# Second product of a fused Mamba-2 and feed-forward kernel: operands exchanged, so that its outputs come by tokens

## Chip, core and metric

The kernel runs on one core of one Trainium2 chip. The metric is device microseconds of one execution, the median of repeated runs: 374.59 us before the change (three runs, 374.59 to 374.6). Engines are named TensorE (PE in the profile, with PEld for its weight loads), VectorE (DVE), ScalarE (ACT), GpSimd (POOL) and SyncE (SP). A trailing q (SPq, ACTq) is an engine's own instruction queue.

## What is computed

```python
# block 1: mamba2_ssd on x (4, 8, 768, 32), a (4, 8, 768), B and C (4, 8, 768, 16)
#   per chunk:  y = (C B^T * L) x  +  (C state) * decay ;  state = decay * state + sum(B x decay)
x = attn_out.transpose(0, 2, 1, 3).reshape(3072, 256)      # 3072 tokens, d_model 256
# block 2: feed-forward, w_in (256, 2048), w_out (2048, 256), float64 in memory
h = x @ w_in
g = h * (1.0 / (1.0 + np.exp(-1.702 * h)))
out = (g @ w_out).astype(np.float32)
```

The kernel works in fp32. It computes g as Silu(1.702 h), which is 1.702 times too large, and puts the factor 1/1.702 (`1.0 / GELU_SCALE`) into the end of the second product.

## The kernel before

**Groups.** The 3072 tokens are taken in six groups of 512 (NG = 6, numbered 0 to 5 in the code; the change concerns 1 to 5). For each group the Mamba block gives `yT` (features on partitions, tokens along the free dimension), the first product gives `gT[g, j]` for eight blocks j of 256 hidden units, and the second product, `product(g, j)`, accumulates the outputs over the eight blocks. Group 0 uses plain products (`hidden`, `half`, `project_all`), the first product of group 1 is plain too.

**Seven products for eight.** The second product of groups 1 to 5, and the first product of groups 2 to 5, use the Strassen-Winograd scheme: a 2x2 block product made with seven block products. The sums of the operands are made by VectorE: `mix_w` for the weights (kept), `mix_y` for the first product, and `mix_g(g, j)` (lines 699 to 703) for the block `gT[g, j]`, four sums of 128x256 in three instructions. `product` (line 809) then issues seven matmuls per block, numbered by `ORDER`. The weights are the stationary operand (128x128), gT or its sums the moving one, 256 tokens wide. Each accumulator is therefore 128 output features by 256 tokens. The seven lie in one four-bank PSUM area, `area(f"acc{g}")`, of a pool with one buffer. The same buffer is used by `score(p)` (line 538), the matmuls of the Mamba block's scores, whose result VectorE multiplies into the decays with `weigh(p)` (L557).

**Combining.** When a group's products are done, `combine(g)` (line 849) makes the four output blocks: `copies` (one ScalarE instruction, L840, takes two accumulators to SBUF), then five VectorE additions through `plus` (line 846; all additions are told as L847 in the profile, also those of the first product's chains). The result `c` has features on partitions.

**Transposing.** `give(g)` (line 867) turns that result by eight TensorE transposes of 128x128 (`turn_out`, L864) into two PSUM banks of the general pool, lets ScalarE copy them to `ob` with the factor 1/1.702 (L872), and stores 2 x 256 KB through SyncE's queue (L761).

**Order.** Every engine executes its instructions in the order in which the code emits them. The order around the change is written out by hand in strings that `run` (line 1076) executes: "2.1" is step 1 of the first product's chain for block 2 (`first`, L733 and L743; the letters D, T and S are its VectorE and ScalarE steps), "P" is the next single product of the list given, s1 and s2 are scores, w1 and w2 their weighings, y1 and y2 the `finish` of a Mamba pair, M0 to M2 are mixings. In line 1121 the last products of the group before are interleaved with the first chains of the next group, and `C` is `combine(g - 1)`. In lines 1136 and 1137 the scores s1 follow; `give` stands after w1. In group 5, which has no more Mamba work, `give(4)` stands at line 1155, after the run.

**Closing stretch.** `end(5, 5)` (line 876) does the last three blocks of group 5, ordered by accumulator, so that the combining runs beside the products; the last accumulator's products are split into two halves of 128 tokens, to let the last additions begin. Then three sets of transposes, three scalings (L912, L915 on ScalarE, L918 on VectorE) and three stores (L761, and L883 on two queues).

Of the kernel before, what the change touches and what calls it, by code (L numbers as in the profile page):

```python
# [8 lines left out]
FP32 = mybir.dt.float32  # L9
# [7 lines left out]
P = 128  # L17
# [18 lines left out]
def kernel(  # L36
# [450 lines left out]
    def bank(name):  # L487
        return ps.tile([P, 4 * P], FP32, tag="ff", name=name)
# [49 lines left out]
    def score(p, to=None):  # L538

        s = st[p]  # L540
        BT, CT = s.pop("BT"), s.pop("CT")
        cb = (area(f"cb{p}") if to is None else to).rearrange("p r (k e) -> p r k e", k=2)
        for k, r in [(k, r) for r in range(R) for k in range(2)] if to is not None else [
                (k, r) for k in range(2) for r in range(R)]:
            rows = slice(32 * r, 32 * r + 32)
            nc.tensor.matmul(out=cb[:, r, k], lhsT=BT[rows, k],  # L546
                             rhs=CT[rows, k].rearrange("p q i -> p (q i)"),
                             start=True, stop=True, tile_position=(32 * r, 0),
                             skip_group_check=True)
        s["cb"] = cb  # L550
# [207 lines left out]

    def store(g, half, ob):
        r0 = g * TG + half * HT  # L760
        nc.sync.dma_start(out=out[r0:r0 + HT, :].rearrange("(k p) d -> p k d", p=P), in_=ob)  # L761

    def out_tile(g, half):
        return ffn.tile([P, 2, DM], FP32, tag="ob", name=f"ob{g}_{half}", bufs=2)
# [17 lines left out]

    mixed_w, mixed_g, acc, done = {}, {}, {}, {}

    def mix_w(n):

# [17 lines left out]

    ORDER = (0, 1, 5, 4, 2, 3, 6)

    def product(g, j, only=ORDER, cols=slice(0, HT)):
        if j == 0 and g not in acc:  # L810
            if g < NG - 1:
                a = area(f"acc{g}").rearrange("p r (t e) -> p (r t) e", t=2)
                acc[g] = [a[:, i] for i in range(7)], a
            else:

                areas.close()
                last = ctx.enter_context(
                    tc.tile_pool(name="last", bufs=1, space=bass.MemoryType.PSUM))
                tiles = [last.tile([P, 2, HT], FP32, name=f"acc{g}_{i}") for i in range(4)]
                acc[g] = [tiles[i // 2][:, i % 2] for i in range(7)], tiles  # L820
        B = gT[g, j].rearrange("p i (t e) -> p i t e", t=2)
        T = mixed_g[g, j]
        A, S = w_out[:, 2 * j:2 * j + 2], mixed_w[j]

        terms = ((A[:, 0, :P], B[:, 0, 0]), (A[:, 1, :P], B[:, 1, 0]), (S[:, 1], T[:, 2]),
                 (S[:, 0], T[:, 0]), (S[:, 2], T[:, 1]), (S[:, 3], B[:, 1, 1]),
                 (A[:, 1, P:], T[:, 3]))
        for i in only:
            lhsT, rhs = terms[i]
            nc.tensor.matmul(out=acc[g][0][i][:, cols], lhsT=lhsT, rhs=rhs[:, cols],  # L830
                             start=(j == 0 and i in (0, 2, 5, 6)), stop=(j == NF // 2 - 1),
                             skip_group_check=True)

    def copies(g):
        u = ffn.tile([P, 4, HT], FP32, tag="gT", name=f"u{g}", bufs=6)
        c = ffn.tile([P, 2, 2, HT], FP32, tag="gT", name=f"c{g}", bufs=6)
        done[g] = u, c

        if g < NG - 1:
            nc.scalar.activation(u[:, 0:4:3], acc[g][1][:, 0:4:3], AF.Copy)  # L840
        else:
            nc.scalar.activation(u[:, 0], acc[g][0][0], AF.Copy)
            nc.scalar.activation(u[:, 3], acc[g][0][3], AF.Copy)
        return u, c

    def plus(o, v, w):
        nc.vector.tensor_tensor(out=o, in0=v, in1=w, op=ALU.add)  # L847

    def combine(g):


        u, c = copies(g)
        a = acc[g][1]
        plus(u[:, 2], a[:, 2], u[:, 0])
        plus(u[:, 1:3], a[:, 3:5], u[:, 2:3].to_broadcast([P, 2, HT]))
        plus(c[:, 1, 1], u[:, 2], u[:, 3])
        plus(c[:, 0], a[:, 1:6:4], u[:, 0:2])
        plus(c[:, 1, 0], a[:, 6], u[:, 2])

    def turn_out(g, t, blocks, o, ks=range(2)):  # L860

        for i in blocks:
            for k in ks:
                nc.tensor.transpose(out=o[:, k, i * P:(i + 1) * P],  # L864
                                    in_=done[g][1][:, i, t, k * P:(k + 1) * P], identity=ident)

    def give(g):
        for t in range(2):
            o = bank(f"oT{g}_{t}").rearrange("p (k e) -> p k e", k=2)
            turn_out(g, t, range(2), o)  # L870
            ob = out_tile(g, t)
            nc.scalar.activation(ob, o, AF.Copy, scale=1.0 / GELU_SCALE)  # L872
            store(g, t, ob)
        done.pop(g)

    def end(g, j0):

        def products(i, cols=slice(0, HT)):
            for j in range(j0, NF // 2):
                product(g, j, (i,), cols)  # L880

        def put(k0, k1, i, ob, queue):
            queue.dma_start(  # L883
                out=out[g * TG + HT + k0 * P:g * TG + HT + k1 * P, i * P:(i + 1) * P].rearrange(
                    "(k p) d -> p k d", p=P), in_=ob[:, k0:k1])

        _, p2, p6, p5, p7, p3, p4 = acc[g][0][:7]
        products(0)
        products(3)
        u, c = copies(g)  # L890
        u2, u4, u3 = u[:, 2], u[:, 1], c[:, 1, 0]
        products(4)
        products(2)
        plus(u2, p6, u[:, 0])
        plus(u4, p5, u2)
        products(6)
        plus(u3, p7, u2)
        plus(c[:, 1, 1], u3, u[:, 3])
        products(1)
        plus(c[:, 0, 0], p2, u[:, 0])  # L900
        o = [bank(f"oT{g}_{i}").rearrange("p (k e) -> p k e", k=2) for i in range(3)]
        ob = [ffn.tile([P, 2, TG], FP32, tag="gT", name=f"ob{g}_1_{i}", bufs=6)[:, :, :P]
              for i in range(2)]
        halves = [slice(k * P, (k + 1) * P) for k in range(2)]
        products(5, halves[0])
        plus(c[:, 1, 0], p4, u3)
        plus(c[:, 0, 1, halves[0]], p3[:, halves[0]], u4[:, halves[0]])
        products(5, halves[1])
        plus(c[:, 0, 1, halves[1]], p3[:, halves[1]], u4[:, halves[1]])
        turn_out(g, 0, range(2), o[0])  # L910
        half_out = out_tile(g, 0)
        nc.scalar.activation(half_out, o[0], AF.Copy, scale=1.0 / GELU_SCALE)  # L912
        store(g, 0, half_out)
        turn_out(g, 1, (1,), o[2])
        nc.scalar.activation(ob[1], o[2][:, :, P:], AF.Copy, scale=1.0 / GELU_SCALE)  # L915
        put(0, 2, 1, ob[1], nc.scalar)
        turn_out(g, 1, (0,), o[1])
        nc.vector.tensor_single_scalar(out=ob[0], in_=o[1][:, :, :P], scalar=1.0 / GELU_SCALE,  # L918
                                       op=ALU.mult)
        put(0, 2, 0, ob[0], nc.sync)  # L920


    assert PG == 2
# [152 lines left out]
    def run(g, steps, products=(), **do):  # L1076


        products = iter(products)
        for step in steps.split():  # L1080
            if step == "P":
                product(*next(products))
            elif step in do:
                do[step]()
            else:
                j, i = step.split(".")
                first(g, int(j), i)
        assert next(products, None) is None

    def seven(g, j):  # L1090
        return [(g, j, (i,)) for i in ORDER]
# [17 lines left out]
    for g in range(2, NG):  # L1109
# [23 lines left out]

        if more:

            run(g, "2.1 1.S 1.4 1.3 2.6 2.5 2.2 2.7 1.T s1 2.D 2.S w1 give 2.4 3.1 2.3 3.5 2.T M0 3.6 "
                "s2 w2 y1 refill 3.7 3.2 3.D along 4.1 P P 3.4 P 3.S 4.6 P 3.3 4.5 3.T M1 P P y2 4.7 P 4.2 4.D M2",
                seven(g, 0), s1=lambda: score(n), w1=lambda: weigh(n), give=lambda: give(g - 1),
                s2=lambda: score(n + 1), w2=lambda: weigh(n + 1), y1=lambda: finish(n),
                refill=refill, along=along, y2=lambda: finish(n + 1), M0=lambda: mix_g(g, 0), M1=lambda: mix_g(g, 1),  # L1140
                M2=lambda: mix_g(g, 2))
            if most:
                decay(chunks[0])
        else:
            run(g, "2.1 1.S 1.4 1.3 2.6 2.5 2.2 2.7 1.T 2.D M0 3.1 3.5 2.S 2.4 3.6 2.3 3.2 3.7 2.T 3.D M1",
                M0=lambda: mix_g(g, 0), M1=lambda: mix_g(g, 1))
# [5 lines left out]
        k = NF // 2 - 1  # L1152
        run(g, f"P {k}.S P {k}.4 P P {k}.3 {k}.T P P P", seven(g, 4))
        if not more:
            give(g - 1)
            for j in range(k - 1, k + 1):
                mix_g(g, j)
            break
# [37 lines left out]
```

## Time and profile before

| | before |
|---|---|
| time, median of 3 | 374.59 us |
| span of the profiled execution | 373.0 us |
| transposes of outputs, L864 | 40, in five runs of eight, starting at 157.42, 214.46, 271.50, 357.13 and 367.77 us |
| passes of the second product, L830 | 566 (two per fp32 matmul) |
| additions with 128x512 at L847, gT<-Y,ac | 32, mean 691 ns |
| copies of transposed outputs, ScalarE L872 | eight in four pairs, a pair takes 1.08 us |
| stores of 256 KB, out_dram<-ob | 11, median 2.4 us from issue to landing |
| DMA, mean over the span | 79 GB/s |

How to read it: a matmul in fp32 appears as two weight loads and two MATMUL records. Matmuls are pipelined, so the duration of a record (its latency) is longer than the distance between two starts, and "busy" is no measure of how well the array is used. The times at the left of a timeline are microseconds from the start of the span; a group's first number is the start of its first instruction and the second the length from there to the end of the last. In brackets stands how long the engine sat idle, and who released it.

### The profile page before, as it was taken

The numbers are of one execution on the slowest core, as the hardware profiler recorded it, in microseconds if no ns is written. First come the engines' busy times: TensorE is split into PE (matmuls) and PEld (weight loads), VectorE is DVE, ScalarE is ACT, GpSimd is POOL, SyncE is SP. The second block draws the span as 40 slices with busy tenths as digits, with TensorE's granted clock in tenths as the row PEclk, the third lists the DMA queues.
The fourth block names the chain that finished last, engine by engine and source line by source line (L and its number), as shares of the span: only waits on it lengthen the run. The fifth ranks groups of instructions, "written<-read, shape, count | busy, mean of one in ns | idle before, by whom it ended". The sixth has DMA issues, their size and how long they took to land.

```text
span 373.0 us, 5764 instructions
## 1 busy us (share of the span) xinstructions
PE 364.5 (98%) x2278; PEld 285.1 (76%) x2278; DVE 267.6 (72%) x439; ACT 151.9 (41%) x337; POOL 10.9 (3%) x34
## 2 busy tenths in 40 slices
PE   8999999999999999999999999999999999999995
PEld 3674468885467588778888788888878888888884
DVE  4999999998879976587886475888484355464443
ACT  5678661402331123553433554433554331554320
POOL 4200000100000010000000000000000000000000
PEclk9999999999999999999999999999999999999999
DMA  9997799706856110086300073000010000000011
GB/s 151 240 335 128 241 215 140 239 18 106 191 143 112 58 42 0 2 155 128 113 2 1 0 128 100 0 2 0 0 58 2 0 3 1 0 2 0 0 58 56
DMA packets 85794, 29.56 MB, mean 79 GB/s; under 512 B 75720, under 2 KB 79240, under 8 KB 85768
## 3 DMA queue, kind: packets, MB, share of 16 engines
q1 hardware_dynamic: 83320, 28.81, 32.8%
q10 hardware_dynamic: 2448, 0.39, 0.6%
q8 instruction: 18, 0.29, 0.3%
q14 instruction: 8, 0.07, 0.1%
HBM read 25.95 MB, written 3.24 MB: 78 GB/s over the span
## 4 chain that ended last, share of the span: by engine, by line
PE 91%; DVE 5%; ACT 2%; DMA 1%; issue 1%; ACTq 0%; DVEq 0%
PE acc L830 33%; PE X L733 13%; PE h L661 13%; PE Y L743 10%; PE o L773 8%; PE cb L546 3%; PE y L619 3%; DVE c L847 2%; PE y L610 2%; PE h L675 1%; PE ab L462 1%; PE tp L498 1%; DVE u L847 1%; PE oT L864 1%; ACT L L481 1%; PE A L574 1%
## 5 line engine op out<-in xcount | busy, mean ns | idle before, releaser
L830 PE MATMUL acc<-mg,mw 128*128 128x256 f32 x240 | 66.0, 379 | 0.0
L847 DVE TENSOR_TENSOR gT<-Y,ac 128x512 f32<-128x512 f32 x32 | 22.1, 691 | 44.3 <-PE Y L743 42.4
L738 ACT ACTIVATE ac<-X 128x256 f32<-128x256 f32 x64 | 24.5, 383 | 66.5 <-PE X L733 66.5
L830 PEld LDWEIGHTS acc<-mg,mw 128*128 128x128 f32 x240 | 45.6, 190 | 6.2
L661 PE MATMUL h<-yT,w_in 128*128 128x512 f32 x112 | 49.9, 595 | 0.0
L710 ACT ACTIVATE gT<-gT 128x512 f32<-128x512 f32 x64 | 33.3, 520 | 28.2 <-DVE gT L847 27.8
L830 PE MATMUL acc<-gT,w_out 128*128 128x256 f32 x160 | 43.8, 380 | 0.0
L347 DVE TENSOR_TENSOR_SCAN L<-a,idents 128x1024 f32<-128x1024 f32 x18 | 41.1, 2283 | 0.0
L733 PE MATMUL X<-my,mi 128*128 128x256 f32 x128 | 38.7, 384 | 0.0
L661 PEld LDWEIGHTS h<-yT,w_in 128*128 128x128 f32 x112 | 20.8, 190 | 23.4 <-issue 21.4
L830 PEld LDWEIGHTS acc<-gT,w_out 128*128 128x128 f32 x160 | 30.2, 190 | 5.5 <-issue 1.4
L847 DVE TENSOR_TENSOR gT<-Y,b 128x256 f32<-128x256 f32 x32 | 13.5, 422 | 26.7 <-PE Y L743 26.4
L664 ACT ACTIVATE gT<-h 128x512 f32<-128x512 f32 x28 | 16.6, 596 | 39.4 <-PE h L661 39.3
L773 PE MATMUL o<-w_out,gT 128*128 128x256 f32 x128 | 29.0, 382 | 0.0
L701 DVE TENSOR_TENSOR mg<-gT 128x512 f32<-128x512 f32 x40 | 27.3, 682 | 0.0
L733 PEld LDWEIGHTS X<-my,mi 128*128 128x128 f32 x128 | 23.7, 190 | 4.3 <-issue 1.2
L773 PEld LDWEIGHTS o<-w_out,gT 128*128 128x128 f32 x128 | 23.8, 190 | 4.1 <-issue 1.1
L557 DVE TENSOR_TENSOR L<-L,cb 128x2048 f32<-128x2048 f32 (+1 forms) x12 | 25.3, 2107 | 1.7 <-PE cb L546 1.6
L830 PE MATMUL acc<-gT,mw 128*128 128x256 f32 (+1 forms) x86 | 24.1, 369 | 0.4 <-DVE c L847 0.4
L830 PE MATMUL acc<-mg,w_out 128*128 128x256 f32 x80 | 23.5, 379 | 0.0
L641 ACT ACTIVATE yT<-y 128x256 f32<-128x256 f32 x22 | 7.2, 381 | 35.6 <-PE y L619 35.3
L733 PE MATMUL X<-yT,w_in 128*128 128x256 f32 x64 | 19.3, 383 | 0.0
(144 smaller groups left out, 540.5 us busy)
## 6 DMA issues: line engine op xcount, KB each, us to landing
a<-scratch SPq DMA_DIRECT2D x18, 512.0 KB, 5.6
bits<-in_moe_w_out_dram SPq DMA_DIRECT2D x4, 1024.0 KB, 7.3
x<-in_x_dram SPq DMA_DIRECT2D x24, 128.0 KB, 3.5
out_dram<-ob SPq DMA_DIRECT2D x11, 256.0 KB, 2.4
bits<-in_moe_w_in_dram SPq DMA_DIRECT2D x4, 512.0 KB, 5.8
bits<-in_moe_w_in_dram SPq DMA_DIRECT2D x2, 1024.0 KB, 9.4
b<-in_B_dram SPq DMA_DIRECT2D x24, 64.0 KB, 3.5
c<-in_C_dram SPq DMA_DIRECT2D x22, 64.0 KB, 2.5
```

Source lines behind the costliest of these rows:

```text
L347: nc.vector.tensor_tensor_scan(out=Ls[p][:, k].rearrange("p r q i -> p (r q i)"), data0=ra[n], data1=idents.rearrange("p h i -> p (h i)"), ...
L557: nc.vector.tensor_tensor(out=Lv[:, k], in0=Lv[:, k], in1=cb.rearrange("p r k e -> p k r e")[:, k], op=ALU.mult)
L661: nc.tensor.matmul(out=h, lhsT=w_in[:, k, f * P:(f + 1) * P], rhs=yT[g][:, k], start=(k == 0), stop=(k == NK - 1))
L664: nc.scalar.activation(gT[g, j][:, i], h, AF.Silu, scale=GELU_SCALE)
L701: nc.vector.tensor_tensor(out=t[:, 0:2], in0=B[:, :, 1], in1=B[:, 0], op=ALU.subtract)
L710: nc.scalar.activation(o, i, AF.Silu, scale=GELU_SCALE)
L733: nc.tensor.matmul(out=s["X"], lhsT=lhsT, rhs=rhs, start=i == "1", stop=i == "4", skip_group_check=True)
L738: nc.scalar.activation(copy, s["X"], AF.Copy)
L743: nc.tensor.matmul(out=o, lhsT=lhsT, rhs=rhs, start=s.pop("new", False), stop=i != "5", skip_group_check=True)
L773: nc.tensor.matmul(out=o[k // 2][:, k % 2], lhsT=gT[g, f // 2][:, f % 2, k * P:(k + 1) * P], rhs=w_out[:, f], start=(f == 0 and k % 2 == 0 ...
L830: nc.tensor.matmul(out=acc[g][0][i][:, cols], lhsT=lhsT, rhs=rhs[:, cols], start=(j == 0 and i in (0, 2, 5, 6)), stop=(j == NF // 2 - 1), ...
L847: nc.vector.tensor_tensor(out=o, in0=v, in1=w, op=ALU.add)
```

## The change

In groups 1 to 5 the two operands of each second product change places: a block of 128 tokens of gT (or of its sums) becomes the stationary operand, and the 128 columns of w_out (or its sums) the moving one. Each product of 256 moving columns thus becomes two of 128. The accumulators, and so the combined outputs, have tokens on partitions, as the output in memory has. So the transposes, their copies and the tiles for them go away; the result of the combining is stored directly. The factor 1/1.702 goes into the copies of `copies` (as ScalarE's scale) and into the additions that read PSUM (`scaled`, a scalar_tensor_tensor in place of a tensor_tensor). The order of the additions in `combine` changes by one: the sum that reads no PSUM comes last. In `end` the split into halves goes, the block of the last accumulator that is ready first is stored earlier, and the first half of the group is stored ahead of the last products.

```diff
@@ -758,7 +758,9 @@
     def store(g, half, ob):
         r0 = g * TG + half * HT
-        nc.sync.dma_start(out=out[r0:r0 + HT, :].rearrange("(k p) d -> p k d", p=P), in_=ob)
+        o = out[r0:r0 + HT, :]
+        nc.sync.dma_start(out=o.rearrange("(k p) d -> p k d", p=P) if len(ob.shape) == 3 else
+                          o.rearrange("(k p) (c d) -> p k c d", p=P, c=2), in_=ob)
     def out_tile(g, half):
         return ffn.tile([P, 2, DM], FP32, tag="ob", name=f"ob{g}_{half}", bufs=2)
@@ -806,7 +808,7 @@
     ORDER = (0, 1, 5, 4, 2, 3, 6)
-    def product(g, j, only=ORDER, cols=slice(0, HT)):
+    def product(g, j, only=ORDER):
         if j == 0 and g not in acc:
             if g < NG - 1:
                 a = area(f"acc{g}").rearrange("p r (t e) -> p (r t) e", t=2)
@@ -826,98 +828,81 @@
                  (S[:, 0], T[:, 0]), (S[:, 2], T[:, 1]), (S[:, 3], B[:, 1, 1]),
                  (A[:, 1, P:], T[:, 3]))
         for i in only:
-            lhsT, rhs = terms[i]
-            nc.tensor.matmul(out=acc[g][0][i][:, cols], lhsT=lhsT, rhs=rhs[:, cols],
-                             start=(j == 0 and i in (0, 2, 5, 6)), stop=(j == NF // 2 - 1),
-                             skip_group_check=True)
+            w, h = terms[i]
+            for k in range(2):
+                cols = slice(k * P, (k + 1) * P)
+                nc.tensor.matmul(out=acc[g][0][i][:, cols], lhsT=h[:, cols], rhs=w,
+                                 start=(j == 0 and i in (0, 2, 5, 6) and k == 0),
+                                 stop=(j == NF // 2 - 1), skip_group_check=True)
     def copies(g):
         u = ffn.tile([P, 4, HT], FP32, tag="gT", name=f"u{g}", bufs=6)
-        c = ffn.tile([P, 2, 2, HT], FP32, tag="gT", name=f"c{g}", bufs=6)
-        done[g] = u, c
+
+        c = ffn.tile([P, 2, 2, DM], FP32, tag="gT", name=f"c{g}", bufs=6)
         if g < NG - 1:
-            nc.scalar.activation(u[:, 0:4:3], acc[g][1][:, 0:4:3], AF.Copy)
+            nc.scalar.activation(u[:, 0:4:3], acc[g][1][:, 0:4:3], AF.Copy,
+                                 scale=1.0 / GELU_SCALE)
         else:
-            nc.scalar.activation(u[:, 0], acc[g][0][0], AF.Copy)
-            nc.scalar.activation(u[:, 3], acc[g][0][3], AF.Copy)
-        return u, c
+            nc.scalar.activation(u[:, 0], acc[g][0][0], AF.Copy, scale=1.0 / GELU_SCALE)
+            nc.scalar.activation(u[:, 3], acc[g][0][3], AF.Copy, scale=1.0 / GELU_SCALE)
+        return u, c.rearrange("p t k (c e) -> p c t k e", c=2)
     def plus(o, v, w):
         nc.vector.tensor_tensor(out=o, in0=v, in1=w, op=ALU.add)
+    def scaled(o, v, w):
+
+        nc.vector.scalar_tensor_tensor(out=o, in0=v, scalar=1.0 / GELU_SCALE, in1=w,
+                                       op0=ALU.mult, op1=ALU.add)
+
+    def by_k(t):
+        return t.rearrange("p (k e) -> p k e", k=2)
+
     def combine(g):
         u, c = copies(g)
         a = acc[g][1]
-        plus(u[:, 2], a[:, 2], u[:, 0])
-        plus(u[:, 1:3], a[:, 3:5], u[:, 2:3].to_broadcast([P, 2, HT]))
-        plus(c[:, 1, 1], u[:, 2], u[:, 3])
-        plus(c[:, 0], a[:, 1:6:4], u[:, 0:2])
-        plus(c[:, 1, 0], a[:, 6], u[:, 2])
-
-    def turn_out(g, t, blocks, o, ks=range(2)):
-
-        for i in blocks:
-            for k in ks:
-                nc.tensor.transpose(out=o[:, k, i * P:(i + 1) * P],
-                                    in_=done[g][1][:, i, t, k * P:(k + 1) * P], identity=ident)
-
-    def give(g):
+        scaled(u[:, 2], a[:, 2], u[:, 0])
+        scaled(u[:, 1:3], a[:, 3:5], u[:, 2:3].to_broadcast([P, 2, HT]))
+        scaled(c[:, 1, 0], by_k(a[:, 6]), by_k(u[:, 2]))
+        split = "p t (k e) -> p t k e"
+        scaled(c[:, 0], a[:, 1:6:4].rearrange(split, k=2), u[:, 0:2].rearrange(split, k=2))
+        plus(c[:, 1, 1], by_k(u[:, 2]), by_k(u[:, 3]))
         for t in range(2):
-            o = bank(f"oT{g}_{t}").rearrange("p (k e) -> p k e", k=2)
-            turn_out(g, t, range(2), o)
-            ob = out_tile(g, t)
-            nc.scalar.activation(ob, o, AF.Copy, scale=1.0 / GELU_SCALE)
-            store(g, t, ob)
-        done.pop(g)
+            store(g, t, c[:, :, t].rearrange("p c k e -> p k c e"))
     def end(g, j0):
-        def products(i, cols=slice(0, HT)):
+        def products(i):
             for j in range(j0, NF // 2):
-                product(g, j, (i,), cols)
-
-        def put(k0, k1, i, ob, queue):
-            queue.dma_start(
-                out=out[g * TG + HT + k0 * P:g * TG + HT + k1 * P, i * P:(i + 1) * P].rearrange(
-                    "(k p) d -> p k d", p=P), in_=ob[:, k0:k1])
-
-        _, p2, p6, p5, p7, p3, p4 = acc[g][0][:7]
+                product(g, j, (i,))
+
+        def put(i, queue):
+            queue.dma_start(out=out[g * TG + HT:(g + 1) * TG, i * P:(i + 1) * P].rearrange(
+                "(k p) d -> p k d", p=P), in_=c[:, i, 1])
+
+        _, p2, p6, p5, p7, p3, p4 = (by_k(t) for t in acc[g][0][:7])
         products(0)
         products(3)
         u, c = copies(g)
-        u2, u4, u3 = u[:, 2], u[:, 1], c[:, 1, 0]
+        u1, u4, u2, u5 = (by_k(u[:, i]) for i in range(4))
         products(4)
         products(2)
-        plus(u2, p6, u[:, 0])
-        plus(u4, p5, u2)
+        scaled(u2, p6, u1)
+        scaled(u4, p5, u2)
         products(6)
-        plus(u3, p7, u2)
-        plus(c[:, 1, 1], u3, u[:, 3])
+        scaled(u2, p7, u2)
+        plus(c[:, 1, 1], u2, u5)
+        put(1, nc.scalar)
         products(1)
-        plus(c[:, 0, 0], p2, u[:, 0])
-        o = [bank(f"oT{g}_{i}").rearrange("p (k e) -> p k e", k=2) for i in range(3)]
-        ob = [ffn.tile([P, 2, TG], FP32, tag="gT", name=f"ob{g}_1_{i}", bufs=6)[:, :, :P]
-              for i in range(2)]
-        halves = [slice(k * P, (k + 1) * P) for k in range(2)]
-        products(5, halves[0])
-        plus(c[:, 1, 0], p4, u3)
-        plus(c[:, 0, 1, halves[0]], p3[:, halves[0]], u4[:, halves[0]])
-        products(5, halves[1])
-        plus(c[:, 0, 1, halves[1]], p3[:, halves[1]], u4[:, halves[1]])
-        turn_out(g, 0, range(2), o[0])
-        half_out = out_tile(g, 0)
-        nc.scalar.activation(half_out, o[0], AF.Copy, scale=1.0 / GELU_SCALE)
-        store(g, 0, half_out)
-        turn_out(g, 1, (1,), o[2])
-        nc.scalar.activation(ob[1], o[2][:, :, P:], AF.Copy, scale=1.0 / GELU_SCALE)
-        put(0, 2, 1, ob[1], nc.scalar)
-        turn_out(g, 1, (0,), o[1])
-        nc.vector.tensor_single_scalar(out=ob[0], in_=o[1][:, :, :P], scalar=1.0 / GELU_SCALE,
-                                       op=ALU.mult)
-        put(0, 2, 0, ob[0], nc.sync)
+        scaled(c[:, 1, 0], p4, u2)
+        scaled(c[:, 0, 0], p2, u1)
+        store(g, 0, c[:, :, 0].rearrange("p c k e -> p k c e"))
+        products(5)
+        scaled(c[:, 0, 1], p3, u4)
+        put(0, nc.sync)
     assert PG == 2
@@ -1133,9 +1118,9 @@
         if more:
-            run(g, "2.1 1.S 1.4 1.3 2.6 2.5 2.2 2.7 1.T s1 2.D 2.S w1 give 2.4 3.1 2.3 3.5 2.T M0 3.6 "
+            run(g, "2.1 1.S 1.4 1.3 2.6 2.5 2.2 2.7 1.T s1 2.D 2.S w1 2.4 3.1 2.3 3.5 2.T M0 3.6 "
                 "s2 w2 y1 refill 3.7 3.2 3.D along 4.1 P P 3.4 P 3.S 4.6 P 3.3 4.5 3.T M1 P P y2 4.7 P 4.2 4.D M2",
-                seven(g, 0), s1=lambda: score(n), w1=lambda: weigh(n), give=lambda: give(g - 1),
+                seven(g, 0), s1=lambda: score(n), w1=lambda: weigh(n), 
                 s2=lambda: score(n + 1), w2=lambda: weigh(n + 1), y1=lambda: finish(n),
                 refill=refill, along=along, y2=lambda: finish(n + 1), M0=lambda: mix_g(g, 0), M1=lambda: mix_g(g, 1),
                 M2=lambda: mix_g(g, 2))
@@ -1152,7 +1137,6 @@
         k = NF // 2 - 1
         run(g, f"P {k}.S P {k}.4 P P {k}.3 {k}.T P P P", seven(g, 4))
         if not more:
-            give(g - 1)
             for j in range(k - 1, k + 1):
                 mix_g(g, j)
             break
```

More of the change, by code (lines that the diff above doesn't have):

```diff
@@ L781, in project_all @@
             store(g, half, ob)
-    mixed_w, mixed_g, acc, done = {}, {}, {}, {}
+    mixed_w, mixed_g, acc = {}, {}, {}
     def mix_w(n):
```

## The prediction

> **What bounds the kernel now.** I read the page's busy shares first, then the waits, the chain in order of time, and the timeline of TensorE and of VectorE around the two places where the change removes work. The page:
>
> ```profile
> PE 364.5 (98%) x2278; PEld 285.1 (76%) x2278; DVE 267.6 (72%) x439; ACT 151.9 (41%) x337; POOL 10.9 (3%) x34
> PE 91%; DVE 5%; ACT 2%; DMA 1%; issue 1%; ACTq 0%; DVEq 0%
> L830 PE MATMUL acc<-mg,mw 128*128 128x256 f32 x240 | 66.0, 379 | 0.0
> ```
>
> TensorE is the bound: it is busy 98% of the span and is 91% of the chain. So each nanosecond per pass that the exchange adds is paid, and work taken from ScalarE is worth nothing by itself. The mean of 379 ns is the latency of one pipelined pass, not its price; the price is the distance between starts. The timeline of TensorE at the end gives it for each width:
>
> ```profile
> 359.31 4.05 PE L830 MATMUL acc<-mg,mw 128*128 128x256 f32 x18
> 365.78 0.83 PE L830 MATMUL acc<-gT,mw 128*128 128x128 f32 x6
> 357.13 1.04 PE L864 MATMUL oT<-ident,c 128*128 128x128 f32 x8
> ```
>
> An fp32 product is two passes. Eighteen passes of 256 columns: (4.05 - 0.379) / 17 = 216 ns each, 432 a product. Six passes of 128 columns (the last group's halves, before the change): the last has a latency of 0.275, so (0.83 - 0.275) / 5 = 111 ns. Single starts in the trace are 109, 111, 112, 112, 111 ns apart. Transposes: (1.04 - 0.273) / 7 = 110 ns. So 128 columns cost slightly more than half of 256.
>
> The other places where TensorE does not run are after a combining. The chain, in order of time, around group 1's outputs:
>
> ```profile
> 152.50 0.45 PE acc L830 x2
> ...
> 153.03 0.61 ACT u L840
> ...
> 154.84 1.37 DVE c L847 x3
> 156.21 0.14 issue
> 156.35 1.15 PE cb L546 x16
> 157.49 1.02 PE oT L864 x8
> ```
>
> The scores (L546) write the one PSUM area that the accumulators held, so they wait for the last read of it, ending at 156.20.
>
> **What the skill says.** TensorE: Matmul & The Clock Gate, section LDWEIGHTS, prices a weight load by its columns, P/1.2: 107 ns for 128. Its section Back-to-back issue gap says that loads and matmuls together set the spacing. The trace agrees: with 256 columns a load hides under 216 ns; with 128 the pace is 109 to 112 ns, hardly above the load. VectorE: DVE Perf Modes, section on the TRN2 errata, has (N+151)/0.96 for an fp32 tensor_tensor, 424 ns at 256 and 691 at 512; this trace has 424 and 691. It states no price for scalar_tensor_tensor. PSUM — Partial Sum Buffer, table of terms, has TensorE and VectorE not use one bank at once; the trace has TensorE standing still 0.55 us beyond its pace at 366.34, until VectorE has read half of that bank.
>
> **Part 1, the exchange (adds).** Each product becomes two of 128 columns, four passes. By the starts above, a product alone between wider ones costs 109 + 111 + 112 + 112 = 444 ns (+12.5 over the measured 431.5), one followed by another product 4 x 112 = 448 (+16). Of 280 products 259 lie before the closing stretch; 94 of these are followed by another product. 94 x 16 + 165 x 12.5 = 3.6 us, all on TensorE's path. Ends of the unknown: 109 each (436, as for transposes; 259 x 4.5 = 1.2 us) and 116 (464; 8.4 us). I take 3.6, since the halves are the same kind of instruction with the same operands, their roles exchanged. The number of instructions doubles to one per 56 ns in the worst stretch; between 15.3 and 22.9 us TensorE started 128 matmuls and 126 loads in 7.6 us, 30 ns each, so issue should not bound.
>
> **Part 2, scale in the combining (moved).** Four of five additions become scalar_tensor_tensor. Nearest rows: L173 (128x512) has 714 ns mean and L184 688, against 691 of tensor_tensor; L596 (128x128, with a per-partition scalar) has 350 against 288. I take no difference; the upper end is 60 ns each, 0.24 us a group. The scale on ScalarE's copies is free (L912, with a scale, 0.60, as L840 without). What moves is the order: the sum that doesn't read PSUM goes last. Before, the area was free after starts of 0.46 + 0.72 + 0.35 + 0.60 and a last 0.42; after, 0.46 + 0.72 + 0.34 and a last 0.69: 0.32 us earlier. The wait before the scores gives that back, in groups 2 to 4 (three times); group 5 has no scores, and its sum of VectorE work is unchanged.
>
> **Part 3, the transposes inside the run (removed).** Eight passes in each of groups 2 to 4, 0.93 us from the first one's start to the next matmul's. Whether TensorE keeps that depends on VectorE, in the stage that follows:
>
> ```profile
> 157.55 2.29 DVE L557 TENSOR_TENSOR L<-L,cb 128x2048 f32<-128x2048 f32 x1 [0.42 <-PE cb L546]
> 159.94 0.42 DVE L847 TENSOR_TENSOR gT<-Y,b 128x256 f32<-128x256 f32 x1
> 160.28 0.68 DVE L701 TENSOR_TENSOR mg<-gT 128x512 f32<-128x512 f32 x1
> ...
> 161.90 2.29 DVE L557 TENSOR_TENSOR L<-L,cb 128x2048 f32<-128x2048 f32 x1
> 164.44 0.69 DVE L847 TENSOR_TENSOR gT<-Y,ac 128x512 f32<-128x512 f32 x1 [0.25 <-PE Y L743]
> ```
>
> Call the first scores' start S (156.35). The first weighing starts at S + 1.20. The second scores need the area back at its end, S + 3.49. TensorE, without the transposes, could start them at S + 3.43: about 0.1 of wait, not 0.9. Behind the first weighing VectorE has an addition and a mixing (1.96 us from 159.94 to 161.90), all of it ready, so the second weighing starts at S + 1.20 + 2.21 + 1.96 = S + 5.37 and ends at S + 7.66. The group's first product needs the area that this weighing reads. TensorE started it at 164.60 = S + 8.25 and could now at about S + 7.5; VectorE allows S + 7.73. So of 0.93 us 0.52 remain, and 0.41 becomes a new wait for the second weighing. Gain with part 2: 3 x (0.32 + 0.52) = 2.5 us. Bounds: 3 x 0.2 if the new additions are slow and the wait is longer, 3 x 1.25 if nothing binds. Behind that waiting product only TensorE's own queue is held; ScalarE has time (41%).
>
> Group 5's transposes lie at 357.13, counted in part 4. ScalarE's copies (1.08 us a group) and their outputs cost nothing today and give nothing: ScalarE is off the path. The stores leave from the sums themselves, earlier; they wait in SyncE's queue ahead of loads that were issued after the stores before, too. Same bytes, DMA nearly idle there.
>
> **Part 4, the end.** Today from 357.13, the start of group 5's transposes, to the last store's issue:
>
> ```profile
> 367.00 0.94 PE L830 MATMUL acc<-gT,mw 128*128 128x128 f32 x6 [0.39 <-DVE c L847]
> 367.77 1.04 PE L864 MATMUL oT<-ident,c 128*128 128x128 f32 x8
> ...
> 368.84 0.42 DVE L918 TENSOR_SCALAR ob<-oT 128x256 f32<-128x256 f32 x1 [0.58 <-PE oT L864]
> ...
> 369.54 0.42 SPq L883 DMA_DIRECT2D out_dram<-ob  x1
> ```
>
> That is 12.41 us. Afterwards: 18 products x 0.448 = 8.06; twelve passes of the last three products, the last starting 11 x 0.112 = 1.23 later; its latency 0.275; 0.04 to VectorE; one sum of 0.42; 0.05 to the issue: 10.08. Gain 2.3 us (1.9 to 2.6). The mixings for group 5's last blocks keep VectorE until 359.5 and are wanted from about 358.5 on, first parts first, so nothing should wait. The rest of the span after that issue, 3.46 us, is the store itself and stays.
>
> **Sum.** 3.57 - 2.52 - 2.33 = -1.28: 374.59 - 1.28 = 373.3 us.
>
> **The rivals.** *The passes cost 109 to 110 ns and weight loads hide altogether*: then 3.6 shrinks to 1.2 and the time is about 371. For it: the transposes hold 109.5. Against: the halves settle at 112. *A wait replaces the transposes*: VectorE's chain of two weighings and a mixing sets the stage, and only 0.2 us a group is won; 374.6 + 3.6 - 0.6 - 2.3 = 375.3, no change. For it: VectorE is without a gap from 159.94 to 164.19. Against: the 0.32 us at the front moves that whole chain. *The exchanged product is slower than the halves show*: loads taken from gT, mg while VectorE and ScalarE write there, or the doubled number of instructions, bring a pass to 116 to 120 ns; with 116, 8.4 - 2.5 - 2.3 = +3.6, so 378; with 120 (48.5 ns a product, 12.6 us), 382. For it: only twelve such passes stand in the trace, in two short runs that TensorE's queue may have held ready. Against: the 30 ns an instruction seen early in the kernel.
>
> **How the numbers follow.** Forecast 0.52, loads hidden 0.12, wait in the place of the transposes 0.22, slower passes 0.14. The range takes in the forecast with its bounds, the near end of the hidden loads and the second rival: 371.8 to 375.4. Faster by over 0.2% (below 373.84): all of the hidden loads and most of the forecast, 0.60. Same: the rest of the forecast and most of the second rival, 0.25. Slower: 0.15.
>
> **What would show it.** In the changed profile: starts of L830's passes 111 to 112 ns apart; the scores' wait after a combining 0.3 us shorter; a new wait of 0.3 to 0.5 us of the group's first product for L557; the last store issued about 10.1 us after the last pass of group 5's run; no row of L864. Starts over 114 ns apart, or a wait of 0.9 us at either scores or first product, would make it wrong upward; starts of 109 downward.

## The result and the profile after

The changed kernel takes 372.54 us (median of six runs), against 374.75 us of the kernel before in the same comparison. The ratio is 0.9933, with a 95% interval of 0.9912 to 0.9953: 2.2 us faster by medians. A second comparison gave 372.21 us and 0.9934 (0.9922 to 0.9946). The profiled spans are 373.0 us before and 370.5 us after.

Busy shares, shares of the chain, and the costliest group of the second product, from the page after:

```profile
PE 363.9 (98%) x2792; PEld 300.3 (81%) x2792; DVE 266.7 (72%) x437; ACT 146.9 (40%) x327; POOL 10.8 (3%) x34
PE 92%; DVE 5%; ACT 1%; DMA 1%; issue 0%; ACTq 0%; DVEq 0%
L834 PE MATMUL acc<-mw,mg 128*128 128x128 f32 x480 | 67.7, 275 | 0.0
```

TensorE is still the bound. It has 514 passes more than before (the second product has 1120 for 566, the 40 transposes are gone), and its weight loads rose from 76% to 81% of the span. The busy time of matmuls hardly moved; as before, it isn't the price. The price is in the distance between starts. The timeline of TensorE in the closing stretch:

```profile
359.17 4.18 PE L834 MATMUL acc<-mw,mg 128*128 128x128 f32 x36
```

(4.18 - 0.276) / 35 = 111.5 ns from pass to pass, over 36 in a row; the same products took 18 passes of 216 before. Between two wider operations a product takes 444 ns in the trace, as was worked out.

The chain, in order of time, after group 1's last products:

```profile
156.31 0.45 PE X L733 x2
156.75 0.04 issue
156.79 1.18 PE cb L546 x16
157.97 0.02 issue
158.00 2.30 DVE L L557
160.29 0.04 issue
160.34 1.15 PE cb L546 x16
```

The ScalarE copy and the additions that stood in this chain before the scores are no longer in it: the last read of the accumulators now ends about when TensorE arrives. In their place VectorE's first weighing (L557) stands between the two sets of scores. The waits show the same, for the second scores and for the group's first product (total us, times, longest us):

```profile
PEld cb L546 <- DVE L L557: 1.3, 3, 0.4
PEld acc L834 <- DVE L L557: 0.7, 3, 0.4
```

These are times in which the weight loads stood still; the matmuls hide part of them. Before the second scores the starts of matmuls lie 208 ns beyond the pace in all three groups (93 before the change, the cost of going over to the scores' shape). Before the group's first product they lie 144 ns beyond it in group 2 alone, and not at all in groups 3 and 4 (0 before in all). The second pass of that product also starts late, 213 ns after the first in group 2 and 133 in the others, where 109 is the pace. So the new wait of the first product is 0.25 us in group 2 and 0.02 in groups 3 and 4. There TensorE arrives later by itself: it has eight passes at L610 between the scores and the product where group 2 has four, 0.22 us more.

The table follows the stages in both traces. S is the start of a group's first scores, P that of its first second product.

| stage | before | after | difference |
|---|---|---|---|
| first second product (group 1) to S of group 2 | 44.99 | 45.49 | +0.50 |
| of this, the wait before the scores | 0.555 | 0.218 | -0.34 |
| S to P, groups 2, 3, 4 | 8.25, 8.48, 8.47 | 7.60, 7.68, 7.68 | -0.65, -0.80, -0.79 |
| P to the next group's S, twice | 48.79, 48.56 | 49.39, 49.09 | +0.60, +0.53 |
| of this, the wait before the scores | 0.496, 0.498 | 0.158, 0.159 | -0.34 each |
| P of group 4 to group 5's closing stretch | 78.24 | 79.61 | +1.37 |
| closing stretch to the last store's issue | 12.41 | 10.04 | -2.37 |
| last store's issue to the end | 3.46 | 2.67 | -0.79 |

The waits in the table contain the 0.09 us of going over to the scores' shape. Taking the waits out of the rows, the products cost 0.84 + 0.94 + 0.87 + 1.37 = 4.0 us more; 0.14 of this is the late second pass of the first products (0.10 in group 2, 0.02 in groups 3 and 4). The scores' shorter waits give 1.0, the removed transposes inside the run 2.2, the closing stretch 2.4, and the last store 0.8, which had not been forecast. Sum: -2.4 us, and 0.06 at the start.

The end in the timeline after:

```profile
365.87 1.50 PE L834 MATMUL acc<-mw,gT 128*128 128x128 f32 x12
...
367.41 0.42 DVE L856 SCALAR_TENSOR_TENSOR c<-acc,u 128x256 f32<-128x256 f32 x1 [0.91 <-PE acc L834]
367.87 0.37 SPq L883 DMA_DIRECT2D out_dram<-c  x1
```

One sum and one store follow the last pass; the standstill between the two halves, the transposes and the scaling are gone. By the two traces, the 2.4 us of the closing stretch are 0.9 for the transposes at its start, 0.6 for the standstill (the last twelve passes take 1.23 us from the first start to the last, 1.88 before) and 1.1 from the last pass's start to the issue (0.77 for 1.88), less 0.3 for the narrower passes. No run takes this stretch apart.

### The profile page after: what moved, and what is told of

Its sections match the earlier page's. It is cut to its first block, busy times and chain, and to the rows that moved or that the text cites. A ratio compares the mean times of both kernels' runs of the same rounds, so it can differ in the third digit from the quotient of the medians.

```text
span 370.5 us, 6778 instructions
## 1 busy us (share of the span) xinstructions
PE 363.9 (98%) x2792; PEld 300.3 (81%) x2792; DVE 266.7 (72%) x437; ACT 146.9 (40%) x327; POOL 10.8 (3%) x34
## 4 chain that ended last, share of the span: by engine, by line
PE 92%; DVE 5%; ACT 1%; DMA 1%; issue 0%; ACTq 0%; DVEq 0%
PE acc L834 34%; PE X L733 14%; PE h L661 13%; PE Y L743 10%; PE o L775 8%; PE cb L546 3%; PE y L619 3%; DVE L L557 2%; PE y L610 2%; PE h L675 1%; PE ab L462 1%; PE tp L498 1%; ACT L L481 1%; PE A L574 1%; DMA az<-in_a_dram 1%; DVE c L856 0%
## 5 line engine op out<-in xcount | busy, mean ns | idle before, releaser
L834 PEld LDWEIGHTS acc<-mw,mg 128*128 128x128 f32 x480 | 65.9, 192 | 3.5
L834 PE MATMUL acc<-mw,mg 128*128 128x128 f32 x480 | 67.7, 275 | 0.0
L834 PEld LDWEIGHTS acc<-w_out,gT 128*128 128x128 f32 x320 | 43.4, 192 | 4.2 <-issue 1.4
L834 PE MATMUL acc<-w_out,gT 128*128 128x128 f32 x320 | 45.1, 276 | 0.0
L733 PE MATMUL X<-my,mi 128*128 128x256 f32 x128 | 38.9, 385 | 0.0
L557 DVE TENSOR_TENSOR L<-L,cb 128x2048 f32<-128x2048 f32 (+1 forms) x12 | 25.3, 2106 | 0.6 <-PE cb L546 0.4
L834 PE MATMUL acc<-mw,gT 128*128 128x128 f32 x160 | 24.3, 277 | 0.0
L834 PE MATMUL acc<-w_out,mg 128*128 128x128 f32 x160 | 24.0, 275 | 0.0
L834 PEld LDWEIGHTS acc<-mw,gT 128*128 128x128 f32 x160 | 22.8, 192 | 1.5
L834 PEld LDWEIGHTS acc<-w_out,mg 128*128 128x128 f32 x160 | 22.8, 192 | 1.2
L733 PEld LDWEIGHTS X<-my,mi 128*128 128x128 f32 x128 | 20.2, 191 | 2.0 <-issue 1.2
```

Of the source, the lines that this page charges most:

```text
L557: nc.vector.tensor_tensor(out=Lv[:, k], in0=Lv[:, k], in1=cb.rearrange("p r k e -> p k r e")[:, k], op=ALU.mult)
L733: nc.tensor.matmul(out=s["X"], lhsT=lhsT, rhs=rhs, start=i == "1", stop=i == "4", skip_group_check=True)
L834: nc.tensor.matmul(out=acc[g][0][i][:, cols], lhsT=h[:, cols], rhs=w, start=(j == 0 and i in (0, 2, 5, 6) and k == 0), stop=(j == NF // 2 ...
```

## The experiments

The theory: TensorE's starts set the time; narrow passes cost 4 us, and three removals give it back with more. Each step has a rival, named in the expectation. The first comparison has the changed kernel itself in it (372.21 us), with the transposes put back, the order of the sums and the plain additions; their differences are against that. The other runs were timed in two later comparisons, in which the kernel before took 374.85 and 374.82 us, for 374.65 in the first. Where they alter the changed kernel, their difference from 372.21 us is read together with the stages of the traces.

### Base of the first comparison

> The changed kernel itself, once more, beside the runs that alter one thing in it: 372.3 to 372.8 us, -0.6% against before. It is the base for the next three.

It took 372.21 us, and every stage of the table came out as in the first profile, within 0.02 us.

### The narrowing alone

The kernel before, with the moving operand cut and the operands not exchanged:

```diff
-            nc.tensor.matmul(out=acc[g][0][i][:, cols], lhsT=lhsT, rhs=rhs[:, cols], ...)
+            for k in range(cols.start, cols.stop, P):
+                nc.tensor.matmul(out=acc[g][0][i][:, k:k + P], lhsT=lhsT, rhs=rhs[:, k:k + P], ...)
```

> The kernel before with nothing but the narrowing: each second product in two of 128 moving columns, operands not exchanged, transposes and all else kept. Theory (a pass of 128 columns costs 109 to 112 ns whichever operand is stationary): 444 to 446 ns a product instead of 432 and 2 ns on the next wider pass, 277 products: +4.0 us, about 378.6. Rival 1 (the roles matter, loads from the tiles that VectorE and ScalarE write are the dearer ones): under +2. Rival 2 (the doubled number of instructions costs more where all else of the old kernel is kept): over +6.

378.99 us against 374.85: +4.1 (ratio 1.0113, 1.0099 to 1.0127). From the first second product to S it is 45.82 us, 0.83 more than before; the changed kernel has 0.84 more there, once its shorter wait is taken out. Up to the closing stretch the narrowing costs 3.85 us in all, and the changed kernel 4.0 less the 0.14 of the late second passes. So the cost is that of the narrower pass; which operand is stationary makes no difference that shows, nor does it matter that gT is written by other engines. The remaining 0.28 us of the run's 4.1 lies in the closing stretch. The closing stretch of this run, from TensorE's timeline:

```profile
363.77 4.18 PE L831 MATMUL acc<-mg,mw 128*128 128x128 f32 x36
```

The 36 passes take 4.18 us, as in the changed kernel.

### What sets 112 ns

In the changed kernel the stationary operand is halved for blocks 1 to 7:

```diff
-                nc.tensor.matmul(out=acc[g][0][i][:, cols], lhsT=h[:, cols], rhs=w,
+                m = P if j == 0 else P // 2
+                nc.tensor.matmul(out=acc[g][0][i][:m, cols], lhsT=h[:, k * P:k * P + m], rhs=w,
```

> The changed kernel with stationary operands of 64 columns for blocks 1 to 7; the other half of each block's tokens is left out of the sums. The moving operand stays at 128 columns. Theory (the weight load of 128 columns sets the last 3 ns of a pass): starts 109 ns apart instead of 112 and no 2 ns on the next pass: 970 passes x 2.5 = -2.4 us against the changed kernel, 370. Rival (the pass itself takes 112 in fp32): no difference, 372.5.

416.91 us, about 45 slower: neither theory had that. The timeline of TensorE shows two things:

```profile
200.40 0.70 PE L743 MATMUL Y<-yT,w_in 128*128 128x256 f32 x2
201.03 0.65 PE L835 MATMUL acc<-w_out,mg 128*64 128x128 f32 x4
201.52 1.04 PE L835 MATMUL acc<-w_out,gT 128*64 128x128 f32 x8
202.49 0.70 PE L733 MATMUL X<-my,w_in 128*128 128x256 f32 x2
```

Within the eight passes the starts lie (1.04 - 0.273) / 7 = 110 ns apart, 109 in single starts: the step from 112 to 109 is there, with loads of half the columns. The record of a load falls from 191 to 136 ns. That supports the load as what sets the last 3 ns; but the run also halves the rows of the output that a pass writes, and doesn't tell the two apart. And at each change between 128 and 64 stationary columns TensorE loses time. The two wide passes at 200.40 take 0.63 us to the next start, where two take 0.43 elsewhere; single starts at such a place in the same trace (from 250.50 us) are 309, 160, 203 and 320 ns, where 216, 109, 109 and 216 are the pace. That is 0.34 us for one product between two wide operations. The trace has 142 such stretches of one product or more, which makes about 48 us, less some 2 us for the faster passes: enough for the loss. The product of the changed kernel keeps 128 x 128 and so never pays it.

### The transposes put back

```diff
-            run(g, "... 2.D 2.S w1 2.4 3.1 2.3 3.5 2.T M0 3.6 "
+            run(g, "... 2.D 2.S w1 idle 2.4 3.1 2.3 3.5 2.T M0 3.6 "
+        def idle():
+            t = bank("idle")
+            for i in range(8):
+                nc.tensor.transpose(out=t[:, i % 4 * P:(i % 4 + 1) * P], in_=ident, identity=ident)
```

> The changed kernel with eight transposes of the identity put back at the old place in groups 2 to 4, their result read by nobody. Theory (most of the removed transposes' time is kept, a part went into waits for the two weighings): the wait before the second scores falls from 208 to about 95 ns and that of the group's first product from 144 to 0, so each group pays 0.6 us instead of 0.93: +1.7 us against the changed kernel, 374.2. Rival 1 (TensorE alone sets this stage): 3 x 0.93 = +2.8, 375.3. Rival 2 (VectorE sets it, the transposes lay in a wait): +0.3, 372.8.

374.09 us, +1.9 (ratio to before 0.9981, 0.9975 to 0.9987). S to P is 8.17, 8.39 and 8.39 us, 0.57, 0.71 and 0.71 more than in the changed kernel, together 2.0. So of 0.93 us for eight transposes about 0.7 came back in groups 3 and 4. Of the rest 0.12 lies in what is now the wait before the second scores, and 0.10 in a change of shape: the first two wide passes after the scores start 320 ns apart when they follow them directly, and 219 when the transposes stand between. In group 2 a further 0.14 lies in the wait of the first product, and its late second pass gives 0.10 back after P. The expectation had taken group 2's wait for all three groups. The second rival, that the transposes had lain in a wait, falls; the first, that nothing binds, falls by 0.9 us. The timeline of this run shows the second scores with no standstill beyond the change of shape: 0.52 us from the start of two passes of 216 ns, so 0.09.

```profile
160.45 0.59 PE L733 MATMUL X<-my,mi 128*128 128x256 f32 x2
...
160.97 1.15 PE L546 MATMUL cb<-CT,BT 32*128 32x256 f32 x16
```

### The order of the sums

```diff
+        plus(c[:, 1, 1], by_k(u[:, 2]), by_k(u[:, 3]))
-        scaled(c[:, 1, 0], ...)
         scaled(c[:, 0], ...)
-        plus(c[:, 1, 1], by_k(u[:, 2]), by_k(u[:, 3]))
+        scaled(c[:, 1, 0], ...)
```

> The changed kernel with the sum that reads no PSUM third again, as it was before. Theory (the scores wait for the last read of the accumulators): the wait before the scores grows by 0.33 us in groups 2 to 4, all that follows in the group shifts with it: +1.0 us, 373.5. Rival (another release ends that wait, or the stage after it has slack that takes it up): under +0.3.

373.33 us, +1.1. The way to S is 45.82 us for 45.49, and the two later ones are longer by 0.33 and 0.32; S to P is unchanged. The chain of this run has the additions in it again:

```profile
155.86 0.42 DVE c L852
156.28 0.94 DVE c L856 x2
157.23 0.14 issue
157.36 1.15 PE cb L546 x16
```

So the change of one line in the order is worth 1.0 of the 2.2 us. Nothing in it needs the exchange of the operands; what it is worth in the kernel before was not run.

### Plain additions

```diff
-        nc.vector.scalar_tensor_tensor(out=o, in0=v, scalar=1.0 / GELU_SCALE, in1=w, ...)
+        nc.vector.tensor_tensor(out=o, in0=v, in1=w, op=ALU.add)
```

> The changed kernel with plain additions in place of the scaled ones; the factor 1/1.702 is left out of the sums, so the outputs lack it in part. Theory (a scalar_tensor_tensor with a constant costs what a tensor_tensor costs, 0.42 and 0.69 us): within 0.1 us of the changed kernel. Rival (60 ns more for each): four sums in the chain before the scores, 0.24 us in each of three groups and 0.1 at the end, so 0.8 us less: 371.7.

372.45 us, 0.24 more in the median than the changed kernel, where at most 0.1 was expected. But every stage from the first second product on is within 0.01 us of the changed kernel's; the profiled run started that product 0.29 us later, ahead of any scaled sum. The scaled sum costs no more than the plain one: two sums of 128x256 take 1.02 us from the first's start either way (VectorE's timelines of this run, and of the changed kernel):

```profile
155.84 1.02 DVE L856 TENSOR_TENSOR c<-acc,u 128x256 f32<-128x256 f32 x2
```

```profile
155.62 1.02 DVE L856 SCALAR_TENSOR_TENSOR c<-acc,u 128x256 f32<-128x256 f32 x2
```

(The second of the two covers a shape of 512; the row names the first.)

### The last store

After the result it was open why the last store came 0.8 us sooner to the end. The issues' median times from issue to landing, for the last 128 KB before and after:

```profile
out_dram<-ob SPq DMA_DIRECT2D x1, 128.0 KB, 2.6
```

```profile
out_dram<-c SPq DMA_DIRECT2D x1, 128.0 KB, 1.8
```

Before, three stores (256, 128 and 128 KB) are issued within 0.5 us; after, at 365.30, 366.53 and 367.87 us. In the kernel before, two of the three were left out:

```diff
-        store(g, 0, half_out)
-        put(0, 2, 1, ob[1], nc.scalar)
```

> The kernel before with two of the last three stores left out (the first half of group 5 and one block of its second half, which are not written). Theory (the last store lands late because the three are in flight together): issue to landing of the last one falls from 2.6 to 1.8 us, and its issue comes up to 0.25 us earlier since SyncE's queue is free: -0.8 to -1.1 us, about 373.6. Rival (a store of 128 KB from ob takes 2.6 us by its form): -0.25 at most.

373.94 us, -0.9 (ratio 0.9974, 0.9965 to 0.9984). The last store of this run:

```profile
368.71 0.42 DVE L916 TENSOR_SCALAR ob<-oT 128x256 f32<-128x256 f32 x1 [0.58 <-PE oT L864]
...
369.16 0.37 SPq L883 DMA_DIRECT2D out_dram<-ob  x1
```

It leaves 0.03 us after the scaling, where it waited 0.28 behind the other store in SyncE's queue, and the span ends 2.77 us after its issue, for 3.46. The form of the store is the old one; so it was the company that made it late. Whether the store ahead of it in its own queue or the one in the other queue did it, the run doesn't tell.

### Where the rest of the waits could go

```diff
-   2.4 3.1 2.3 3.5 2.T M0 3.6     s2 w2 y1 refill 3.7 3.2 3.D
+   2.4 3.1 2.3 3.5 2.T 3.6 3.2    s2 w2 M0 y1 refill 3.7 3.D
    # and in group 5: combine(4) after step 1.3 instead of before 2.1
```

> The changed kernel with three things placed anew: the mixing M0 after the second weighing, chain step 3.2 ahead of the second scores, and in group 5 the combining after step 1.3. Theory: the wait of the first product for the second weighing goes (0.14 us and its 0.1 of start, three times), that before the second scores falls by 0.1 (three times), and that of step 3.5 in group 5 goes (0.3 and 0.1): -1.1 us against the changed kernel, 371.4. Rival (the sums that come later now are waited for elsewhere, the first products that use M0 or the chain of block 3): -0.3 or slower than the changed kernel.

373.26 us, slower than the changed kernel by 1.0 where 1.1 less was expected. Where they were made, the first two moves did most of what they should: S to P is 7.42, 7.56 and 7.56, and the second scores wait no longer. Group 2's first product still waits for L557, 80 ns before its start for 144; groups 3 and 4 had next to none to lose. But group 2's P to S grew by 0.57, and group 5's way by 0.84. There the sum of the second chain had to queue behind the combining, and TensorE stood for the bank that it frees (timelines of VectorE and of TensorE):

```profile
327.88 0.41 DVE L852 TENSOR_TENSOR c<-u 128x256 f32<-128x256 f32 x1
328.22 0.68 DVE L852 TENSOR_TENSOR gT<-Y,ac 128x512 f32<-128x512 f32 x1
```

```profile
328.95 0.70 PE L743 MATMUL Y<-yT,mi 128*128 128x256 f32 x2 [0.45 <-DVE gT L852]
```

The next run takes group 5's part back, and moves the decay of rows (`along`) behind M1:

```diff
-   s2 w2 M0 y1 refill 3.7 3.D along 4.1 P P ... 3.T M1 P P y2
+   s2 w2 M0 y1 refill 3.7 3.D 4.1 P P ... 3.T M1 along P P y2
```

> The changed kernel with the mixing M0 after the second weighing and step 3.2 ahead of the second scores, as in the run before, but group 5 left as it was and the decay of rows (two VectorE instructions of 2.3 us together) placed behind M1. Theory (the loss of the run before came from group 5's combining, whose place held up the sums of its first chains, and in group 2 from VectorE's queue ahead of the third chain's sum): first products at S + 7.42 to 7.56 instead of 7.60 to 7.68, no new wait: -0.4 us against the changed kernel, 371.9. Rival (the moves themselves cost what they win): 372.3 or more.

371.73 us (ratio to before 0.992, 0.9906 to 0.9933). S to P stays at 7.42 to 7.56, P to the next S is back at 49.39 and 49.06, group 5 at 79.59. From the first second product to the end it is 258.8 us, against 259.2 of the changed kernel. Then the end:

```diff
+        for k, queue in enumerate((nc.scalar, nc.sync)):
+            products(5, (k,))          # the second half in a free quarter of the last bank
+            scaled(c[:, 0, 1, k], ...) # 128 columns, then its store of 64 KB
```

> The same, and the last accumulator of group 5 split by tokens into two PSUM banks, so that its first half is summed and stored while the second half's products run. Theory (the end is the last pass, one sum, one store): the last sum is of 128 columns (0.29 for 0.42 us) and the last store of 64 KB: -0.3 us more, 371.6. Rival (two stores in flight together at the end delay each other): no gain over the version without it, 371.9.

371.72 us (0.9919, 0.9906 to 0.9933). The trace has the last pass 3.12 us ahead of the end for 3.42, and 258.5 us from the first second product: the 0.3 us is there, but the medians of the two don't show it. By these stages the two versions beat the changed kernel by 0.5 and 0.8 us; the medians, of different comparisons, lie 0.5 below 372.21 us, and the intervals of the ratios overlap with the changed kernel's.

## Why the prediction was right

The forecast was 373.3 us, faster, in a range of 371.8 to 375.4; measured were 372.54. The bound, the price of the passes and the three places of gain were right. The sizes were less so: -1.3 us forecast, -2.2 measured by medians and -2.4 by stages, and a third of that gain, the last store's 0.8, was not in the sum. That the passes cost a little more than forecast drew the number back towards it; that part is luck.

**Part 1, the exchange.** Forecast 3.6, measured 4.0, of which 0.14 belongs to part 3 (the late second passes). The starts taken from twelve passes at the end of the kernel before held for 1120: 444 ns alone, 446 in rows (448 forecast). In the run with the narrowing alone, set beside the kernel before pass by pass, the products themselves cost 3.5 us more and the passes after them 0.4: a further 2 ns falls on the next wider pass (218 for 216), which the sum had left out. The rival of slower passes falls with that, and so does that of hidden loads. The load's 107 ns, on which the prediction's reading rests, is no duration in these traces: the record of a load lasts 190 ns before and 192 after. That is more than the 112 ns from pass to pass, so a load's record is no price either.

**Part 2, the sums.** 0.32 us a group forecast, 0.34 measured, 0.33 when undone; the prediction's own terms add up to 2.55 - 2.21 = 0.34. The scaled sums cost nothing, as assumed from the nearest rows.

**Part 3, the transposes in the run.** Forecast 0.52 a group, measured 0.65, 0.80 and 0.79, or with the late second passes 0.55, 0.78 and 0.77. For group 2, from which it was worked out, the step that named the new bound was right: the second scores and the first product wait for the weighings. Its terms were off both ways: VectorE's chain ended at S + 7.54, not S + 7.66, since the 1.96 us read for the sum and the mixing held about 0.1 in which the second weighing waited for its own scores (1.85 after the change), and the late second pass was not foreseen.

Two things were mis-sized beyond that. Group 2 was taken for all: groups 3 and 4 had 8.48 us from S to P before, not 8.25, and in them TensorE itself comes last and the first product starts at its pace. The wait of 0.3 to 0.5 us named as a sign shows in the weight loads of group 2 (0.38) and not in the others (0.16, hidden under the matmul ahead). And ScalarE's copies of the transposed outputs were put at nothing. The waits of the kernel before have a line for them:

```profile
PEld X L733 <- ACT ob L872: 0.7, 3, 0.2
```

In each of groups 2 to 4 a pass of the first product (L733) started 84 ns beyond the pace there. In the run with the transposes put back but nothing copied it starts at the pace of 216, so the copies cost 0.25 us in all; this gain is in the measured numbers. The rival in which a wait takes the place of all but 0.2 us falls by the same run.

**Part 4, the end.** 10.08 us forecast from the stretch's start to the last issue, 10.04 measured. The step that failed stands in its last sentence: the 3.46 us from issue to end "is the store itself and stays". It fell to 2.67. The trace of before had what was needed: three issues within 0.5 us, so three stores in flight at once. The run with one store shows that this was the cause.

The profiled spans differ by 2.5 us where 1.3 was forecast. Of these 1.2 us the last store is 0.8, part 3 is 0.5, parts 2 and 4 are 0.1 and the start 0.1, less 0.3 for part 1.

## What to carry to other kernels

Read the price of a pass from starts in the trace, for the exact width and shape, before trading widths: here 128 columns cost 112 ns and 256 cost 216, so cutting a moving operand in two was about 3% dearer, and removing a transpose pays for it only where TensorE is not waiting anyway. After work is taken from the bounding engine, recompute who holds the next buffer: of the 2.8 us of transposes taken here inside the run 0.6 went into waits for VectorE and 0.3 into a change of shape, and moving two items gave 0.4 back. Work out such a wait for each group: a few passes more ahead of it decide whether it exists. An engine that is off the path, as ScalarE was here, can still hold a buffer. At the end of a kernel, spread the stores: the last one landed sooner here when it was alone (2.77 us from issue to end for 3.46).

## What was not expected of the hardware

A change of the stationary operand's width between 128 and 64 columns cost about 0.34 us for each product between wider operations, and that run was 45 us slower, though each pass in itself became 3 ns faster. The last store of 128 KB took 2.6 us to land in company and 1.8 where the stores were spread.

The front, whose code is the same in all runs, differs from run to run: the first second product started between 111.2 and 113.3 us in the profiles here, while the stages after it repeat to 0.02 us where their code is the same. A part lies in the loads: the first VectorE instruction that waits for them starts at 3.98 to 4.63 us, released by a landing transfer. The larger part lies in TensorE's own pace in one place, shown here for the changed kernel and for the profile with 113.3 us (the run with a median of 371.73 us, whose profiled execution took 373.8):

```profile
6.15 1.15 PE L462 MATMUL ab<-cum,pick 32*128 32x256 f32 x16 [0.97 <-DVE cum L290]
```

```profile
6.40 2.09 PE L462 MATMUL ab<-cum,pick 32*128 32x256 f32 x16 [0.56 <-DVE cum L290]
```

The 32 passes of L462 take 1.94 us to the next matmul in eight of the twelve profiles, 2.2 to 2.5 in three, and 3.72 in this one, where each set of four follows the last by 0.43 us instead of 0.22. The cause of that is not shown. The stages, which leave the front out, therefore separate versions that the medians don't.
